# Attention with a feed-forward layer on one core: the scores' lower products on 64 rows, in pairs, and the last six products in two parts

## The chip, the cores and the metric

The kernel runs on one core of a Trainium2 chip. The metric is the device time of one execution in microseconds (us). Before the change three runs took 1043.27 to 1043.53 us, with a median of 1043.49.

The core's engines each work through their own queue in program order and wait for one another through semaphores: TensorE (PE; its weight loads are listed apart as PEld), VectorE (DVE), ScalarE (ACT), GpSimd (POOL), and SyncE (SP), which issues the DMAs.

## The reference

```python
# q, k, v: 8 batches x 8 heads x 576 positions x 64, float32
scores = scale * np.matmul(q, k.transpose(0, 1, 3, 2))      # scale = 1/8
mask = block_i >= block_j                                   # blocks of 64 positions
scores = np.where(mask, scores, -1000000000.0)
scores = scores - np.max(scores, axis=-1, keepdims=True)
attn = np.exp(scores)
attn = attn / (np.sum(attn, axis=-1, keepdims=True) + 1e-09)
attn_out = np.matmul(attn, v)
# heads side by side: x is 4608 x 512; w_in 512 x 2048, w_out 2048 x 512
h = x @ w_in
g = h * (1.0 / (1.0 + np.exp(-h)))
out = g @ w_out
```

So it is block-causal attention, and behind it a feed-forward layer (FFN) with a silu, on all 4608 tokens.

## The kernel before, in words

**Precision.** PE multiplies numbers of a rounded type, fp32r. To keep more digits, an operand is split in two: the upper part is the number rounded to fp32r, the lower part is what rounding left out. A product then is a sum of up to four: upper by upper, upper by lower, lower by upper, lower by lower.

**The first 128 queries** of each head are handled ahead, in large groups (classes First and Second; L524, L538, L576, L594), with small unrounded products on 64 rows or 64 columns of the PE array. They stand in the first 125 us, between weight preparation and the first FFN products. `warm` (L434) is filler for PE while the first data arrive.

**The units.** The other 448 queries of a head make one *unit*; there are 64 units, 8 batches by 8 heads. A unit's inputs are q and k transposed, 64 rows (the head dimension) by 448 + 576 columns. `load` fetches them twice, into partitions 0 to 63 and again into 64 to 127 (tile `raw`). `split_hi` (L278, ACT) rounds all of it into `qh`. `split_lo` (L282, POOL) then replaces k's columns in partitions 64 to 127 by k's lower part, so that k has its upper part in the lower half of the rows and its lower part in the upper half (`kk`). It also makes `ql`, the lower part of q, in both halves (L284).

**Scores** (L306, PE). A unit's scores are five areas, one per block of 128 keys (the fifth has 64), listed in `SEG` as (key block, column in the score row, first query, queries): 448, 320, 192, 448 and 64 queries wide, in three PSUM banks (`BANKS`). Each area is two products on all 128 rows: `kk` by `qh`, and `kk` by `ql`. With k's two parts in the two halves of the rows, the first gives upper by upper and lower by upper in one go, the second upper by lower and lower by lower. `QK` sets the order of the areas; an area's two products follow one another.

**Behind the scores** VectorE takes maxima (L250), subtracts them (L336, L338) and, behind ScalarE's exponentials, sums; ScalarE and GpSimd split the exponentials into `ph` and `pl`; PE multiplies them by v (L385), and the result becomes FFN input, again split.

**FFN.** Tokens go in 18 blocks of 256 (`TB`), the 2048 hidden columns in 8 steps of 256. `ffn1` (L618) makes 24 products of 256 columns per step, ScalarE applies silu (L625) and rounds (L631), GpSimd makes the lower part (L636), and `ffn2` (L648) makes 6 products of 512 columns for each half `t` of the block's tokens, summed over the 8 steps in one PSUM bank. In the last step `output` (L656) copies the bank into a tile `ot`, and `store` (L661) sends it to memory through SP.

**The order of the work** is written out by hand: a table of tokens for the start and the first 17 units, then a loop that emits each later unit with a number of FFN products between its parts. PE therefore alternates between a unit's scores, a unit's product with v, and FFN products. The last FFN products run after all units, with nothing beside them.

Of the kernel before, what the change touches and what calls it, by code (L numbers as in the profile page):

```python
# [9 lines left out]
F32 = mybir.dt.float32  # L10
# [4 lines left out]
ALU = mybir.AluOpType  # L15
# [3 lines left out]
B, H, S, D = 8, 8, 576, 64  # L19
DM, DFF = 512, 2048  # L20
P = 128
NQ = S - 2 * D
# [4 lines left out]
NFF = DFF // P  # L27
NSTEP = NFF // 2
TB = 256
CT = DM // P  # L30
NX = 16
EVEN = 4
# [5 lines left out]
SEG = [(0, 0, 0, 448), (2, 448, 128, 320), (3, 768, 256, 192), (1, 960, 0, 448), (4, 1408, 384, 64)]  # L38
COLS = 1472

QK = [0, 1, 3, 2, 4]
PV = [(0, 0, 128), (1, 0, 128), (2, 0, 128), (2, 1, 64), (1, 1, 64), (0, 1, 64), (4, 0, 128), (3, 1, 64), (3, 0, 128)]
BANKS = [(0, 448), (448, 960), (960, 1472)]

# [86 lines left out]
def attn_ffn(ctx: ExitStack, tc: tile.TileContext, qk, v, qk0, v0, qk1, v1, w_in, w_out, out):  # L131
    nc = tc.nc
# [5 lines left out]
    def bank(i):  # L138
        return pS.tile([P, 512], F32, tag=f"S{i}", name=f"S{i}")

    pU = pool("pU", space=PSUM)
    pH = pool("pH", bufs=2, space=PSUM)
    pO = pool("pO", bufs=2, space=PSUM)


    wi = [cp.tile([P, CT, DFF], F32R, name=f"wi{t}") for t in range(2)]
    wo = [cp.tile([P, NFF, DM], F32R, name=f"wo{t}") for t in range(2)]
# [10 lines left out]

    xbuf = cp.tile([P, NX, 2, TB], F32R, name="x")
    x_free = list(range(NX))  # L160
# [3 lines left out]
    ready = set()  # L164
# [96 lines left out]
    class Unit:  # L261
# [17 lines left out]

        def split_lo(u):  # L280

            nc.gpsimd.tensor_tensor(out=u.qh[64:, NQ:], in0=u.raw[64:, NQ:], in1=u.qh[64:, NQ:], op=ALU.subtract)  # L282
            u.ql = sp.tile([P, 512], F32R, tag="ql", name="ql")[:, :NQ]
            nc.gpsimd.tensor_tensor(out=u.ql, in0=u.raw[:, :NQ], in1=u.qh[:, :NQ], op=ALU.subtract)  # L284
            u.kk = u.qh[:, NQ:]
# [9 lines left out]
        def scores(u):  # L295
            banks = [bank(0), bank(1), bank(2)]

            def ps(c, w, r=P):
                i = max(i for i in range(3) if BANKS[i][0] <= c)
                return banks[i][:r, c - BANKS[i][0] : c - BANKS[i][0] + w]  # L300

            u.ps = ps
            for j, c, q0, w in (SEG[i] for i in QK):
                m = min(P, S - j * P)
                for i, qq in enumerate((u.qh, u.ql)):
                    nc.tensor.matmul(u.ps(c, w, m), u.kk[:, j * P : j * P + m], qq[:, q0 : q0 + w], start=i == 0, stop=i == 1)  # L306

        def max(u):
            ttr(Mx[:, :, 0], blocks32(u.ps(0, NQ)), ALU.max)
            for j, c, q0, w in SEG[1:4]:  # L310
                ttr(Mx[:, q0 // 32 + 2 :, j], blocks32(u.ps(c + 64, w - 64)), ALU.max)
                if j == 3:
                    u.half_max(0)
            u.half_max(1)
# [88 lines left out]
        def pieces(u):  # L403

            q = 0
            while q < NQ:
                blk, col = divmod(u.b * NQ + q, TB)
                n = min(TB - col, NQ - q)
                z = 4 + blk, u.h // 2
# [30 lines left out]
    class Early:  # L440
# [33 lines left out]
        def turn(u, k):  # L474
            for c in range(CT):
                nc.tensor.transpose(u.ps[k][:, P * c : P * c + P], u.part(k)[:, P * c : P * c + P], ident)
# [4 lines left out]
        def tiles(u, blk, n):  # L481

            for c in range(CT):
                if (blk, c) not in x_tiles:
# [3 lines left out]
            t = x_tiles[blk, 0]  # L488
            assert [x_tiles[blk, c] for c in range(CT)] == list(range(t, t + CT))
            return xbuf[:, t : t + CT]  # L490

    class First(Early):
# [18 lines left out]
        def scores(u):  # L511
# [6 lines left out]
            for k in range(2):  # L518
                for c in range(CT):
                    for e, b in enumerate(HALF):  # L520
# [19 lines left out]
        def hi(u, n):  # L540
            if n == 0:
                u.x = u.tiles(u.g, TB).rearrange("p c i (k n q) -> p i n k c q", k=2, n=2)
            nc.scalar.copy(u.x[:, 0, n], u.ps[n].rearrange("p (k c q) -> p k c q", k=2, c=CT))
# [61 lines left out]
    hs, gs, outs = {}, {}, {}  # L605

    def ffn1(blk, d, f):
        if f == 0:
            hs[blk, d] = pH.tile([P, 2, TB], F32, tag="h", name="h")
        h = hs[blk, d]  # L610
        n = 0
        for c in range(CT):
            x = xbuf[:, x_tiles[blk, c]]
            w = slice((2 * d + f) * P, (2 * d + f + 1) * P)
            assert x_full[blk, c] == TB, (blk, d, c, x_full[blk, c])
            assert ("in", d, c // 2) in ready
# [21 lines left out]
    def ffn2(blk, d, t):  # L638
        g2 = gs[blk, d]
        if d == 0 and t == 0:  # L640
            outs[blk] = [bank(2), pU.tile([P, DM], F32, tag="U", name="o1")] if blk == 0 else [pO.tile([P, DM], F32, tag="o", name="o") for _ in range(2)]
        o = outs[blk][t]
        tk = slice(t * P, t * P + P)
        n = 0
        for f in range(2):
            assert ("out", d, f) in ready
            for gt, wt in ((0, 0), (0, 1), (1, 0)):
                nc.tensor.matmul(  # L648
                    o, g2[:, gt, f, tk], wo[wt][:, 2 * d + f, :],
                    start=d == 0 and n == 0, stop=d == NSTEP - 1 and n == 5,  # L650
                )
                n += 1

    def output(blk, d, t):
        ot = sp.tile([P, DM], F32, tag="ot", name="ot", bufs=2)
        (nc.vector.tensor_copy if late else nc.scalar.copy)(ot, outs[blk][t])  # L656
        outs[blk][t] = ot

    def store(blk, d, t):
        for i, r, w in rows(blk, t):  # L660
            nc.sync.dma_start(out=out[r : r + w, :], in_=outs[blk][t][i : i + w, :])  # L661

    def rows(blk, t):

        if blk < 4:
            return [(i * D, (blk % 2 * 4 + t * 2 + i) * S + blk // 2 * D, D) for i in range(2)]
        r, i = [], 0
        while i < P:
            b, q = divmod((blk - 4) * TB + t * P + i, NQ)
            w = min(P - i, NQ - q)  # L670
            r.append((i, b * S + 2 * D + q, w))
            i += w
        return r


    steps = [(0, 0)] + [z for d in range(EVEN) for z in ((0, d + 1), (1, d))]
    steps += [(0, d) for d in range(EVEN + 1, NSTEP)] + [(1, d) for d in range(EVEN, NSTEP)]
    steps += [(blk, d) for blk in range(2, B * S // TB) for d in range(NSTEP)]


    work_list = []
    for n in range(len(steps) + LAG):
        now = n < len(steps)
        work_list += [("ffn", ffn1, n, f) for f in range(2) if now]
        if n < LAG:
            work_list += [("silu", silu, n), ("g_hi", g_hi, n), ("g_lo", g_lo, n)]
        else:
            last = steps[n - LAG][1] == NSTEP - 1
            for t in range(2):
                work_list += [("ffn", ffn2, n - LAG, t)] + [("output", output, n - LAG, t), ("store", store, n - LAG, t)] * last  # L690
                if now:
                    work_list += [[("silu", silu, n)], [("g_hi", g_hi, n), ("g_lo", g_lo, n)]][t]
    queues = {k: [z for z in work_list if z[0] == k] for k in ("ffn", "silu", "g_hi", "g_lo", "output", "store")}
    late = []
# [36 lines left out]
    for token in ORDER.split():  # L731
        name, _, method = token.partition(".")
        if name.startswith("warm:"):
            warm(int(name[5:]))
        elif method:
            method, _, k = method.partition(":")
# [5 lines left out]
    n = len(units)  # L742
    for i in range(TABLE, n + 2):
        u = units[i] if i < n else None
        w = units[i - 1] if i <= n else None
# [81 lines left out]
```

## Time and profile before

| | |
|---|---|
| median of 3 runs | 1043.49 us |
| the profiled execution's own time | 1043.46 us |
| its span (first to last instruction) | 1041.7 us |
| PE busy | 1033.4 us, 99% |
| weight loads (PEld) busy | 939.7 us, 90% |
| VectorE, ScalarE, GpSimd busy | 763.5, 749.1, 750.0 us |
| DMA | 79.95 MB, mean 77 GB/s |
| scores (L306), two groups | 90.5 and 84.1 us, 320 products each |
| FFN (L618, L648) | 441.6 and 424.3 us |

In a line of a group, the count follows the x; then come the busy time in us, the mean of one instruction in ns, and the idle time of the engine just before such instructions, with what ended it. In a timeline line the first number is the start in us from the span's start, the second the length, followed by engine, line, operation, output and input names, and the shape; for a matmul the first pair (128\*128) is the rows and columns of the array in use and the second the streamed operand. A matmul's recorded length includes its way through the array, so that lengths overlap; the distance between two starts is what it takes from PE. Times of PEld are those of the weight loads, which may run while PE is busy with the product before.

### The profile page before, as it was taken

How to read it: one execution, taken by the hardware profiler on the slowest of the kernel's cores; microseconds unless marked ns; L12 is line 12 of the kernel's file. 1: busy time of each engine (PE TensorE's matmuls, PEld its weight loads, DVE VectorE, ACT ScalarE, POOL GpSimd, SP SyncE). 2: the span in 40 equal slices, each digit the busy share in tenths (PEclk: the TensorE clock that was granted, in tenths of full speed). 3: DMA queues.
4: the chain of work that ended last, by engine and by line, in shares of the span. 5: the costliest groups of instructions: out<-in, count | busy, mean ns of one | idle time of the engine just before them, and what ended most of it. 6: DMA issues, size and time to landing. Idle time of an engine off the chain costs nothing.

```text
span 1041.7 us, 20247 instructions
## 1 busy us (share of the span) xinstructions
PE 1033.4 (99%) x7176; PEld 939.7 (90%) x7176; DVE 763.5 (73%) x2232; ACT 749.1 (72%) x1194; POOL 750.0 (72%) x726
## 2 busy tenths in 40 slices
PE   8999999999999999999999999999999999999998
PEld 8988899999899999999999999998999999989987
DVE  7998489999978988888878888888888888700000
ACT  5876578898797888787878787878787777722222
POOL 5766579898897878787878787878787878622221
PEclk9999999999999999999999999999999999999999
DMA  8876223222322222222322222222222222000000
GB/s 291 260 247 189 63 75 90 52 67 74 92 50 84 54 54 74 55 77 59 85 56 74 59 75 55 64 64 54 74 54 75 54 74 54 27 1 21 1 21 21
DMA packets 35044, 79.95 MB, mean 77 GB/s; under 512 B 4736, under 2 KB 12928, under 8 KB 34944
## 3 DMA queue, kind: packets, MB, share of 16 engines
q1 hardware_dynamic: 34944, 78.66, 26.9%
q8 instruction: 57, 0.93, 0.4%
q14 instruction: 43, 0.35, 0.1%
HBM read 69.21 MB, written 9.44 MB: 75 GB/s over the span
## 4 chain that ended last, share of the span: by engine, by line
PE 87%; DVE 4%; POOL 3%; ACT 2%; DMA 2%; issue 1%; SPq 0%; DVEq 0%; POOLq 0%; ACTq 0%
PE h L618 35%; PE o L648 35%; PE S L306 8%; PE U L385 8%; DVE S L227 1%; DVE wm L233 1%; DVE S L223 1%; DMA wst<-in_moe_w_in_dram 1%; POOL pl L361 1%; POOL g L636 1%; DMA T<-in_moe_w_in_dram 0%; PE S L648 0%; ACT L625 0%; DMA qkraw<-in_qk_dram 0%; POOL qh L282 0%
## 5 line engine op out<-in xcount | busy, mean ns | idle before, releaser
L618 PE MATMUL h<-x,wi 128*128 128x256 f32 x3456 | 441.6, 282 | 0.9 <-ACT g L625 0.6
L618 PEld LDWEIGHTS h<-x,wi 128*128 128x128 f32 x3456 | 430.2, 189 | 12.7 <-ACT g L625 1.0
L648 PE MATMUL o<-wo,g 128*128 128x512 f32 x1680 | 424.3, 397 | 0.0
L648 PEld LDWEIGHTS o<-wo,g 128*128 128x128 f32 x1680 | 305.9, 188 | 62.6 <-issue 0.2
L361 POOL TENSOR_TENSOR pl<-p,ph 128x448 fp32r<-128x448 f32 (+1 forms) x192 | 226.0, 1202 | 93.9 <-ACT ph L353 93.5
L636 POOL TENSOR_TENSOR g<-g,g 128x512 fp32r<-128x512 f32 x144 | 186.4, 1295 | 119.8 <-ACT g L631 115.2
L250 DVE TRANSPOSE_TENSOR_REDUCE Mx<-S 64x4 f32<-64x128 f32 (+4 forms) x384 | 135.7, 405 | 94.0 <-PE S L306 93.9
L625 ACT ACTIVATE g<-h 128x512 f32<-128x512 f32 x144 | 86.1, 598 | 126.0 <-POOL g L636 74.6
L631 ACT CAST g<-g 128x512 fp32r<-128x512 f32 x144 | 89.3, 620 | 60.1 <-PE o L648 58.2
L250 DVE TRANSPOSE_TENSOR_REDUCE Dx<-p 128x14 f32<-128x448 f32 (+3 forms) x320 | 122.6, 446 | 0.1
L347 ACT ACTIVATE p<-T 128x512 f32<-128x512 f32 (+1 forms) x192 | 105.6, 604 | 9.5 <-POOL ph L363 8.5
L353 ACT CAST ph<-p 128x512 fp32r<-128x512 f32 (+1 forms) x192 | 104.4, 596 | 1.3 <-PE U L385 1.1
L282 POOL TENSOR_TENSOR qh<-qkraw,qh 64x576 fp32r<-64x576 f32 x64 | 91.6, 1431 | 15.8 <-ACT qh L278 7.1
L306 PE MATMUL S<-qh 128*128 128x448 f32 (+3 forms) x320 | 90.5, 296 | 0.0
L625 ACT ACT_TABLE_LOAD x66 | 84.7, 1283 | 1.4 <-PE h L618 0.3
L306 PE MATMUL S<-ql,qh 128*128 128x448 f32 (+3 forms) x320 | 84.1, 307 | 0.0
L347 ACT ACT_TABLE_LOAD x62 | 79.5, 1283 | 1.6 <-DVE Dx L250 0.5
L284 POOL TENSOR_TENSOR ql<-qkraw,qh 128x448 fp32r<-128x448 f32 x64 | 74.1, 1157 | 5.1 <-PE S L594 0.2
L385 PE MATMUL U<-ph,vc 128*128 128x448 f32 (+3 forms) x320 | 74.1, 297 | 0.0
L278 ACT CAST qh<-qkraw 128x1024 fp32r<-128x1024 f32 x64 | 66.9, 1045 | 8.8 <-PE S L306 4.1
L338 DVE TENSOR_TENSOR T<-S,MR 128x256 f32<-128x256 f32 (+2 forms) x192 | 73.0, 406 | 0.0
L293 POOL TENSOR_TENSOR vc<-vraw,vc 128x320 fp32r<-128x320 f32 x64 | 56.2, 878 | 13.3 <-ACT vc L290 12.8
(120 smaller groups left out, 1120.4 us busy)
## 6 DMA issues: line engine op xcount, KB each, us to landing
qkraw<-in_qk_dram SPq DMA_DIRECT2D x128, 256.0 KB, 3.9
vraw<-in_v_dram SPq DMA_DIRECT2D x64, 160.0 KB, 2.3
wst<-in_moe_w_out_dram SPq DMA_DIRECT2D x15, 512.0 KB, 4.6
out_dram<-ot SPq DMA_DIRECT2D x24, 256.0 KB, 2.9
wst<-in_moe_w_in_dram SPq DMA_DIRECT2D x10, 512.0 KB, 5.3
v<-in_v_dram SPq DMA_DIRECT2D x12, 256.0 KB, 5.2
qk<-in_qk_dram SPq DMA_DIRECT2D x8, 384.0 KB, 5.3
T<-in_moe_w_in_dram SPq DMA_DIRECT2D x6, 512.0 KB, 4.5
```

Source lines behind the costliest of these rows:

```text
L250: nc.vector.tensor_reduce(out=out, in_=in_, axis=AX.X, op=op, apply_transpose=True)
L282: nc.gpsimd.tensor_tensor(out=u.qh[64:, NQ:], in0=u.raw[64:, NQ:], in1=u.qh[64:, NQ:], op=ALU.subtract)
L306: nc.tensor.matmul(u.ps(c, w, m), u.kk[:, j * P : j * P + m], qq[:, q0 : q0 + w], start=i == 0, stop=i == 1)
L347: nc.scalar.activation(u.p[:, c:e], T[:, c:e], AF.Exp, scale=SCALE)
L353: nc.scalar.copy(u.ph[:, c:e], u.p[:, c:e])
L361: nc.gpsimd.tensor_tensor(out=u.pl[:, c:e], in0=u.p[:, c:e], in1=u.ph[:, c:e], op=ALU.subtract)
L385: nc.tensor.matmul(U[:m, q0 : q0 + w], u.vc[:, j, :m], (u.ph, u.pl)[pp][:, c : c + w], start=n == 0, stop=n == 8)
L618: nc.tensor.matmul(h[:, f, :], wi[wt][:, c, w], x[:, xt, :], start=n == 0, stop=n == 3 * CT - 1)
L625: nc.scalar.activation(g, hs.pop((blk, d)), AF.Silu)
L631: nc.scalar.copy(g2[:, 0], g)
L636: nc.gpsimd.tensor_tensor(out=g2[:, 1], in0=g, in1=g2[:, 0], op=ALU.subtract)
L648: nc.tensor.matmul(o, g2[:, gt, f, tk], wo[wt][:, 2 * d + f, :], start=d == 0 and n == 0, stop=d == NSTEP - 1 and n == 5,)
```

## The change

It has two parts.

*Scores.* The second product of an area leaves out k's lower part: it multiplies only k's upper part by `ql`, on 64 of the 128 rows. For key blocks 0 and 1 k's upper part now lies in rows 64 to 127 (and the lower part in rows 0 to 63), for blocks 2 to 4 the other way round as before; `split_lo` writes the lower part accordingly, in two instructions. The new `QK` lists (area, part) and puts areas in pairs, one of blocks 0 and 1 with one of blocks 2 and 3: first both upper products on 128 rows, then both lower products, one on the upper 64 rows and the other on the lower 64, into different banks. The last area (64 keys) keeps both products on all rows. Lower by lower is left out of the sum for the first four areas.

*The end.* The last six products of the whole program, 512 columns wide, become six of columns 0 to 255 into the old bank and six of columns 256 to 511 into another. The old bank is copied to `ot` after the first six, and its left half can be stored; the right half's last products are then added by VectorE and stored apart.

```diff
-QK = [0, 1, 3, 2, 4]
+QK = [(0, 0), (1, 0), (0, 1), (1, 1), (3, 0), (2, 0), (3, 1), (2, 1), (4, 0), (4, 1)]
...
         def split_lo(u):
-            nc.gpsimd.tensor_tensor(out=u.qh[64:, NQ:], in0=u.raw[64:, NQ:], in1=u.qh[64:, NQ:], op=ALU.subtract)
+            for r, c in ((slice(0, 64), slice(NQ, NQ + 2 * P)), (slice(64, 128), slice(NQ + 2 * P, 1024))):
+                nc.gpsimd.tensor_tensor(out=u.qh[r, c], in0=u.raw[r, c], in1=u.qh[r, c], op=ALU.subtract)
...
-            for j, c, q0, w in (SEG[i] for i in QK):
+            for i, part in QK:
+                j, c, q0, w = SEG[i]
                 m = min(P, S - j * P)
-                for i, qq in enumerate((u.qh, u.ql)):
-                    nc.tensor.matmul(u.ps(c, w, m), u.kk[:, j * P : j * P + m], qq[:, q0 : q0 + w], start=i == 0, stop=i == 1)
+                r = u.upper(j) if part and m == P else slice(0, P)
+                qq = u.ql if part else u.qh
+                nc.tensor.matmul(u.ps(c, w, m), u.kk[r, j * P : j * P + m], qq[r, q0 : q0 + w], start=part == 0, stop=part == 1)
+
+        def upper(u, j):
+            return slice(64, 128) if j < 2 else slice(0, 64)
...
     def ffn2(blk, d, t):
...
+        split = t and (blk, d) == (NBLK - 1, NSTEP - 1)
+        if split:
+            outs[blk][t] += [(bank(0)[:, :HD], slice(HD, DM))]
+        for i, (o, c) in enumerate(outs[blk][t]):
+            if split and i == 0:
+                o, c = o[:, :HD], slice(0, HD)
...
     def output(blk, d, t):
         ot = sp.tile([P, DM], F32, tag="ot", name="ot", bufs=2)
-        (nc.vector.tensor_copy if late else nc.scalar.copy)(ot, outs[blk][t])
-        outs[blk][t] = ot
+        (o, c), *right = outs[blk][t]
+        (nc.vector.tensor_copy if late else nc.scalar.copy)(ot, o)
+        outs[blk][t] = [(ot, c)]
+        for o, c in right:
+            nc.vector.tensor_tensor(out=ot[:, c], in0=o, in1=ot[:, c], op=ALU.add)
+            outs[blk][t] = [(ot, slice(0, HD)), (ot, c)]

     def store(blk, d, t):
-        for i, r, w in rows(blk, t):
-            nc.sync.dma_start(out=out[r : r + w, :], in_=outs[blk][t][i : i + w, :])
+        for ot, c in outs[blk][t]:
+            for i, r, w in rows(blk, t):
+                nc.sync.dma_start(out=out[r : r + w, c], in_=ot[i : i + w, c])
```

On PE, one unit's scores in the middle of the program stood in this order before; `S_...` is a PSUM bank (three numbers, three banks), and the shape is the output's, keys by queries:

```order
L306 MATMUL S_4660<-qh 128x448
L306 MATMUL S_4660<-ql,qh 128x448
L306 MATMUL S_4661<-qh 128x320
L306 MATMUL S_4661<-ql,qh 128x320
L306 MATMUL S_4662<-qh 128x448
L306 MATMUL S_4662<-ql,qh 128x448
L306 MATMUL S_4661<-qh 128x192
L306 MATMUL S_4661<-ql,qh 128x192
L306 MATMUL S_4662<-qh 64x64
L306 MATMUL S_4662<-ql,qh 64x64
```

The same unit on PE after the change:

```order
L313 MATMUL S_4681<-qh 128x448
L313 MATMUL S_4682<-qh 128x320
L313 MATMUL S_4681<-ql,qh 128x448
L313 MATMUL S_4682<-ql,qh 128x320
L313 MATMUL S_4683<-qh 128x448
L313 MATMUL S_4682<-qh 128x192
L313 MATMUL S_4683<-ql,qh 128x448
L313 MATMUL S_4682<-ql,qh 128x192
L313 MATMUL S_4683<-qh 64x64
L313 MATMUL S_4683<-ql,qh 64x64
```

Still ten products of the same widths; the third and fourth, and the seventh and eighth, are the pairs on 64 rows, each into two banks.

At the end of the program, PE's last products before (`wo_75`, `wo_76` are the two parts of w_out):

```order
L648 MATMUL o<-wo_75,g_12894 128x512 x2
L648 MATMUL o<-wo_76,g_12894 128x512
L648 MATMUL o<-wo_75,g_12894 128x512 x2
L648 MATMUL o<-wo_76,g_12894 128x512
L648 MATMUL o<-wo_75,g_12894 128x512
```

And after the change:

```order
L669 MATMUL o<-wo_75,g_12958 128x512
L669 MATMUL o<-wo_75,g_12958 128x256
L669 MATMUL o<-wo_76,g_12958 128x256
L669 MATMUL o<-wo_75,g_12958 128x256 x2
L669 MATMUL o<-wo_76,g_12958 128x256
L669 MATMUL o<-wo_75,g_12958 128x256
L669 MATMUL S_12982<-wo_75,g_12958 128x256
L669 MATMUL S_12982<-wo_76,g_12958 128x256
L669 MATMUL S_12982<-wo_75,g_12958 128x256 x2
L669 MATMUL S_12982<-wo_76,g_12958 128x256
L669 MATMUL S_12982<-wo_75,g_12958 128x256
```

Six products became twelve of half the width, the later six into another bank.

More of the change, by code (lines that the diff above doesn't have):

```diff
@@ L29 @@
 TB = 256
+NBLK = B * S // TB
+HD = DM // 2
 CT = DM // P
@@ L640, in ffn2 @@
         if d == 0 and t == 0:
-            outs[blk] = [bank(2), pU.tile([P, DM], F32, tag="U", name="o1")] if blk == 0 else [pO.tile([P, DM], F32, tag="o", name="o") for _ in range(2)]
-        o = outs[blk][t]
-        tk = slice(t * P, t * P + P)
[L644 to L652, printed above, removed]
+            new = lambda: pO.tile([P, DM], F32, tag="o", name="o")
@@ new lines, in ffn2 @@
+            whole = slice(0, DM)
+            if blk == 0:
+                outs[blk] = [[(bank(2), whole)], [(pU.tile([P, DM], F32, tag="U", name="o1"), whole)]]
+            else:
+                outs[blk] = [[(new(), whole)] for _ in range(2)]
+        tk = slice(t * P, t * P + P)
+        split = t and (blk, d) == (NBLK - 1, NSTEP - 1)
[4 more added lines that the diff above has]
+                o, c = o[:, :HD], slice(0, HD)
+            n = 0
+            for f in range(2):
+                assert ("out", d, f) in ready
+                for gt, wt in ((0, 0), (0, 1), (1, 0)):
+                    nc.tensor.matmul(
+                        o, g2[:, gt, f, tk], wo[wt][:, 2 * d + f, c],
+                        start=(d == 0 or i > 0) and n == 0, stop=d == NSTEP - 1 and n == 5,
+                    )
+                    n += 1
@@ L677, in attn_ffn @@
     steps += [(0, d) for d in range(EVEN + 1, NSTEP)] + [(1, d) for d in range(EVEN, NSTEP)]
-    steps += [(blk, d) for blk in range(2, B * S // TB) for d in range(NSTEP)]
+    steps += [(blk, d) for blk in range(2, NBLK) for d in range(NSTEP)]
     work_list = []
```

## The prediction

> **What bounds the kernel now.** I read the page of the profile first, then the list of PE's waits, then PE's timeline around one unit's scores in the middle of the run. The page's rows give the span, the busy times, the granted clock, and the scores and what reads them.
>
> ```profile
> span 1041.7 us, 20247 instructions
> PE 1033.4 (99%) x7176; PEld 939.7 (90%) x7176; DVE 763.5 (73%) x2232; ACT 749.1 (72%) x1194; POOL 750.0 (72%) x726
> ...
> PEclk9999999999999999999999999999999999999999
> ...
> L250 DVE TRANSPOSE_TENSOR_REDUCE Mx<-S 64x4 f32<-64x128 f32 (+4 forms) x384 | 135.7, 405 | 94.0 <-PE S L306 93.9
> ...
> L306 PE MATMUL S<-ql,qh 128*128 128x448 f32 (+3 forms) x320 | 84.1, 307 | 0.0
> ```
>
> PE is busy for 99% of the span at full granted clock. A busy PE need not be at its peak, so the waits matter more. VectorE waits 94 us for the scores; the other way round there is nothing: before its scores PE has 0.0 us of idle. All of PE's waits, largest first:
>
> ```profile
> PE idle L434 <- DVE zero L429: 1.0, 1, 1.0
> PE S L576 <- PE h L618: 1.0, 1, 1.0
> PE h L618 <- ACT g L625: 0.6, 1, 0.6
> ```
>
> None is for an input of L306, L385 or L648. So while the 64 units run, PE's own stream sets the time, and each nanosecond that a unit's scores get longer or shorter goes into the span as it is. The other engines, at 72 to 73%, follow.
>
> The price of the scores is read from distances between starts (a matmul's recorded length overlaps the next one's). This is PE's timeline of one unit; column 1 is the start, column 2 the length.
>
> ```profile
> 509.24 0.36 PE L306 MATMUL S<-qh 128*128 128x448 f32 x1
> 509.44 0.36 PE L306 MATMUL S<-ql,qh 128*128 128x448 f32 x1
> 509.64 0.31 PE L306 MATMUL S<-qh 128*128 128x320 f32 x1
> 509.79 0.31 PE L306 MATMUL S<-ql,qh 128*128 128x320 f32 x1
> 509.94 0.36 PE L306 MATMUL S<-qh 128*128 128x448 f32 x1
> 510.14 0.37 PE L306 MATMUL S<-ql,qh 128*128 128x448 f32 x1
> 510.35 0.25 PE L306 MATMUL S<-qh 128*128 128x192 f32 x1
> 510.43 0.28 PE L306 MATMUL S<-ql,qh 128*128 128x192 f32 x1
> 510.55 0.19 PE L306 MATMUL S<-qh 128*64 128x64 f32 x1
> ```
>
> A product of 448 columns takes a slot of 0.20 us, one of 320 takes 0.15, the two of 192 take 0.20 together. The weights come free, as PEld's rows of the same place show: the load for the second product starts with the first product, on the same rows of the array, and is done before its turn.
>
> ```profile
> 509.24 0.19 PEld L306 LDWEIGHTS S<-ql,qh 128*128 128x128 f32 x1
> 509.44 0.19 PEld L306 LDWEIGHTS S<-qh 128*128 128x128 f32 x1
> ```
>
> **What the pairs save.** Of each unit's ten products, four (448 with 320, 448 with 192) now use 64 rows each and can run two at a time. That two halves of the rows do run together is seen in the early blocks, whose products have 64 rows (PE's timeline; S and U of one step are the upper and the lower rows on the same columns):
>
> ```profile
> 6.27 0.22 PE L524 MATMUL U<-qk 64*64 64x64 f32 x1
> 6.31 0.22 PE L524 MATMUL S<-qk 64*64 64x64 f32 x1
> 6.31 0.22 PE L524 MATMUL U<-qk 64*64 64x64 f32 x1
> 6.32 0.22 PE L524 MATMUL S<-qk 64*64 64x64 f32 x1
> 6.33 0.22 PE L524 MATMUL U<-qk 64*64 64x64 f32 x1
> 6.47 0.27 PE L434 MATMUL idle<-zero 128*64 128x64 f32 x1
> ```
>
> Four start within 0.02 us, into two banks, and the group before ended its starts at 6.27: four per 0.06 us. So a pair should cost its longer member. That saves the slot of 320 columns, 0.15, and one of 192. The two 192s take 0.20 together; the one that stays needs about 0.09 (192 of 448 columns of 0.20), so 0.11 goes. Together 0.26 us per unit.
>
> **What the pairs cost.** The order of a unit is now: two products on 128 rows, a pair on 64, two on 128, a pair on 64, then two on 128 again (the 64-key block keeps all rows). That is four changes between 128 and 64 rows per unit, where there was none. The trace has such changes where early blocks stand between FFN products. PE, then PEld, at the first of them, and PE's timeline inside and after its block:
>
> ```profile
> 28.25 0.87 PE L618 MATMUL h<-x,wi 128*128 128x256 f32 x6
> ```
> ```profile
> 29.05 0.85 PEld L576 LDWEIGHTS S<-qk 64*64 64x64 f32 x16
> 30.07 0.41 PEld L618 LDWEIGHTS h<-x,wi 128*128 128x128 f32 x3 [0.17 <-issue]
> ```
> ```profile
> 29.05 0.33 PE L576 MATMUL S<-qk 64*64 64x128 f32 x2
> ```
> ```profile
> 29.43 0.71 PE L576 MATMUL S<-qk 64*64 64x128 f32 x10
> ```
> ```profile
> 30.07 0.38 PE L618 MATMUL h<-x,wi 128*128 128x256 f32 x1
> ```
> ```profile
> L618 PE MATMUL h<-x,wi 128*128 128x256 f32 x3456 | 441.6, 282 | 0.9 <-ACT g L625 0.6
> ...
> L576 PE MATMUL S<-qk 64*64 64x128 f32 x128 | 8.7, 275 | 1.4 <-PE h L618 1.0 <-DVE x L602 0.4
> ```
>
> Six L618 products span 0.87 us; less the last one's 0.28 they start 0.118 apart, the last at 28.84. The next would follow at 28.96. Instead, even the weight load comes only at 29.05: 0.09 late, and not ahead of its product any more. Going back is alike: ten L576 products are five pairs in 0.71 us; less 0.27, pairs start 0.11 apart, the last at 29.87. The next slot is 29.98, but the load starts at 30.07, 0.09 late again, and its product is recorded 0.38 long instead of 0.28: it waits another 0.10 for 128 columns of weights. (Into the block it was 0.32 to 0.27, 0.05, for 64 columns.) So a change costs 0.09 plus the bare weight load, 0.10: **0.19 us**.
>
> Those blocks halve the columns too; is it the rows? The row 6.33 above, with 6.47 behind it, changes rows from 64 to 128 and keeps 64 columns: 0.14 between starts where the slot is 0.06, 0.08 late. So a change of rows alone pays it, though no row of before has exactly 128x128 to 64x128. The Trainium skill ("TensorEngine Tiling (Array Packing)", section Tiling Modes) states that a change of tiling mode, not of tile alone, drains TensorE. It gives no price; the rows just quoted agree, and by that rule all four changes of a unit pay.
>
> Per unit: into and out of the first pair and into the second, 3 x 0.19; out of the second pair the next weights have 64 columns, 0.09 + 0.05 = 0.14. That is 0.71. Less the 0.26 saved: +0.45 us, and times 64 units **+28.8 us**. Nothing hides this, for PE waits for no one. Bounds per unit: if the pairs' two loads expose only 0.05 each, as for L576, 0.35, or 22.4 us. If a pair's members take turns, nothing is saved, 0.71, or 45.4 us.
>
> **The other edits.** GpSimd's subtraction of 64x576 becomes 256 and 320 columns. GpSimd's rows:
>
> ```profile
> L282 POOL TENSOR_TENSOR qh<-qkraw,qh 64x576 fp32r<-64x576 f32 x64 | 91.6, 1431 | 15.8 <-ACT qh L278 7.1
> ...
> L284 POOL TENSOR_TENSOR ql<-qkraw,qh 128x448 fp32r<-128x448 f32 x64 | 74.1, 1157 | 5.1 <-PE S L594 0.2
> ...
> L293 POOL TENSOR_TENSOR vc<-vraw,vc 128x320 fp32r<-128x320 f32 x64 | 56.2, 878 | 13.3 <-ACT vc L290 12.8
> ```
>
> From the last two, 128 columns more cost 279 ns, 2.18 each, so 180 ns are fixed. A second instruction adds 0.18 us per unit, 11.5 us of GpSimd's time, while PE never waits for it and its queue has idle time; at most it moves g's and p's lower parts 0.18 us in a unit that itself grows 0.45. I take 0; without that cover it would be the whole 11.5 us. VectorE gets its first block later by the 320 product's slot and the change (0.15 + 0.19 = 0.34 us), again less than the unit grows, so no new wait forms there.
>
> The end, on PE, ScalarE, SP and, for the price of an add of that shape, VectorE's group:
>
> ```profile
> 1037.63 0.63 PE L648 MATMUL o<-wo,g 128*128 128x512 f32 x2
> ```
> ```profile
> 1038.29 0.58 ACT L656 COPY ot<-o 128x512 f32<-128x512 f32 x1 [0.82 <-PE o L648]
> ```
> ```profile
> L338 DVE TENSOR_TENSOR T<-S,MR 128x256 f32<-128x256 f32 x64 | 26.1, 409 | 0.0
> ```
>
> Now the copy of 0.58 runs beside the last six products (six of 256 columns, 6 x 0.118 = 0.71), and only an add of 256 columns, 0.41, follows the last product. Twelve products of 0.118 (L618's distance) stand for six of 0.23 (448 columns' 0.20 scaled to 512): even. In the row above, two of them end at 1038.26, and the copy follows at once. The gain is 0.17 us; the second store queues behind the first on SP, but the first is issued earlier. I take -0.15, with 0 and -0.5 as ends.
>
> **The sum.** The profiled run took 1043.46 us, 1.76 over its span and 0.03 under the median of 1043.49. 1043.46 + 28.8 - 0.15 = **1072.1 us, said as 1072**.
>
> **The rivals.**
> - *Pairs without drains.* If a change of rows alone on 128 columns costs nothing, each unit saves 0.26: 64 x 0.26 = 16.6 us, 1043.46 - 16.6 - 0.15 = 1026.7 us. It decides from 0.065 us per change (0.26 / 4): below that the kernel gains. For it: these operands are rounded (fp32r), those of L524, L434 and L576 are not, and where rounded products go from 128 to 64 columns, 510.43 to 510.55 in the unit, the distance is 0.12, hardly over the 192 columns' 0.09; changes of shape may be cheap for them. Against it: both halves of the rows must hold their own weights here, as at 6.31, and the way back from that cost 0.08 with the columns unchanged. The Trainium skill's table (same page, section Overview) gives up to twice the speed for a contraction of 64 and deducts nothing for getting there; by it this is the outcome. Chance 0.10.
> - *The pair takes turns.* Two full-width products at the rounded rate write twice as much into PSUM as L524's 64 columns did; if they alternate, drains stay and nothing is saved: 1043.46 + 45.4 - 0.15 = 1088.7 us. Chance 0.09.
> - *Weights slip in under the drain.* Only 4 x 0.09 paid: +0.10 per unit, 6.4 us, 1049.7 us. Against it: loads at 29.05 and 30.07 start with the drain's end. Chance 0.03.
> - *Nothing changes in the array:* 64 rows run as 128 with half idle, in turn and without drain: 1043.3 us. Against it: S and U side by side at 6.31. Chance 0.02.
>
> **The numbers.** The forecast of 1072 holds 0.76, mostly between 1064 and 1078. The range must take in the turn-taking pair to leave out no more than 2 in 10: 1063 to 1089. A difference of 0.2%, about 2 us, is what a measurement of this kernel can tell from none. Faster by more 0.10, same 0.02, slower 0.88.
>
> **What would show it.** In the changed kernel's timeline: loads of a pair starting 0.09 after the last slot, both members within 0.01, the first product behind a pair recorded 0.10 longer, a unit's period 0.45 longer, PE's busy share and PEld's falling a little, and still no wait of PE for another engine. The prediction is wrong if the loads of the pair start with the product ahead of them, if members start 0.15 or more apart, or if PE waits for VectorE or GpSimd.

## The result, and the profile after

The changed kernel takes 1071.2 us (median of 4 runs, 1071.05 to 1072.36), the kernel before 1043.51 beside it. The ratio is 1.0266, 95% interval 1.0254 to 1.0279: 27.7 us slower. The forecast was 1072.

The page of the changed kernel, in the rows that answer to those of before:

```profile
span 1069.3 us, 20315 instructions
PE 1062.4 (99%) x7182; PEld 918.5 (86%) x7182; DVE 765.3 (72%) x2233; ACT 750.6 (70%) x1194; POOL 758.9 (71%) x790
...
PEclk9999999999999999999999999999999999999999
...
L253 DVE TRANSPOSE_TENSOR_REDUCE Mx<-S 64x4 f32<-64x128 f32 (+4 forms) x384 | 136.5, 406 | 117.8 <-PE S L313 117.7
...
L287 POOL TENSOR_TENSOR qh<-qkraw,qh 64x256 fp32r<-64x256 f32 (+1 forms) x128 | 102.9, 804 | 18.5 <-ACT qh L281 9.2
```

PE is still at 99% and at full clock, VectorE waits 118 us for the scores instead of 94, and GpSimd's line has the 11 us more that its second instruction was priced at (102.9 us in L287, 91.6 in L282 before). The busy share of PE hides the loss: a product that waits for its weights is recorded longer and counts as busy. PEld's fall from 90 to 86% is no measure of it either: the two loads of a pair now run side by side (below), which by estimate takes 128 x 0.19 = 24 us out of PEld's busy time (939.7 to 918.5 us). Of the kernels tried below, one_island has 922.2 us of PEld with hardly any loss, and alone has 949.4 with the largest. PE's list of waits, of which these are the first two lines, names no score input:

```profile
PE idle L445 <- DVE zero L440: 1.0, 1, 1.0
PE S L587 <- PE h L629: 1.0, 1, 1.0
```

One unit in the changed kernel, PE's timeline; a row of x2 holds two products, and its shape is the first one's. The last two rows are single products from narrower windows: the first one behind the first pair, and the next unit's first one:

```profile
523.60 0.51 PE L313 MATMUL S<-qh 128*128 128x448 f32 x2
524.04 0.46 PE L313 MATMUL S<-ql,qh 64*128 64x448 f32 x2
524.43 0.56 PE L313 MATMUL S<-qh 128*128 128x448 f32 x2
524.92 0.46 PE L313 MATMUL S<-ql,qh 64*128 64x448 f32 x2
525.32 0.24 PE L313 MATMUL S<-qh 128*64 128x64 f32 x1
525.40 0.22 PE L313 MATMUL S<-ql,qh 128*64 128x64 f32 x1
525.45 0.72 PE L629 MATMUL h<-x,wi 128*128 128x256 f32 x4
...
524.43 0.47 PE L313 MATMUL S<-qh 128*128 128x448 f32 x1
...
536.74 0.36 PE L313 MATMUL S<-qh 128*128 128x448 f32 x1
```

and the weight loads of the same place:

```profile
524.03 0.19 PEld L313 LDWEIGHTS S<-ql,qh 64*128 64x128 f32 x2 [0.25 <-issue]
524.43 0.30 PEld L313 LDWEIGHTS S<-qh 128*128 128x128 f32 x2 [0.21 <-issue]
524.92 0.19 PEld L313 LDWEIGHTS S<-ql,qh 64*128 64x128 f32 x2 [0.20 <-issue]
525.32 0.13 PEld L313 LDWEIGHTS S<-qh 128*64 128x64 f32 x1 [0.21 <-issue]
```

At each of the four changes of rows the load column has a hole of 0.20 to 0.25 us in front of it, marked "issue": in that time PEld waits for nothing that the profile shows. Over all units the profile lists 253 such holes before L313's loads, 54.6 us together, and three more that end with GpSimd: 256, four times 64. Before L306's loads, in the kernel before, it lists none. Going in: the second product started at 523.80 (523.60 + 0.51 - 0.31), its slot ends at 523.95, the load comes at 524.03, 0.08 late. The pair's two loads start together (both fit into 0.19, the length of one) and so do its two products, both done by 524.50; the longer is recorded 0.46 long where 448 columns had 0.36, 0.10 for bare weights. The groups of all units, the members of 448 and of 320 columns, say the same of both:

```profile
L313 PE MATMUL S<-ql,qh 64*128 64x448 f32 x128 | 59.8, 467 | 0.0
L313 PE MATMUL S<-ql,qh 64*128 64x320 f32 x64 | 26.3, 410 | 0.0
```

Before, on 128 rows, these products had means of 365 and 309 ns: each member waits 0.10 us for its weights, none waits for the other. Coming out: 524.04 + 0.10 + 0.20 = 524.34 is the end of the pair's slot, the load comes at 524.43, 0.09 late, and the product behind it has 0.47, another 0.10 or 0.11.

In the kernel before, the unit behind the one that began at 509.24 began here:

```profile
521.93 0.36 PE L306 MATMUL S<-qh 128*128 128x448 f32 x1
```

So a unit took 521.93 - 509.24 = 12.69 us and now takes 536.74 - 523.60 = 13.14: +0.45, and 64 x 0.45 = 28.8 us. The loss lies among the units: from the first to the last start of their upper products it was 771.1 us (120.6 to 891.7), and it is 798.9 now (120.7 to 919.6).

### The profile page after: what moved, and what is told of

It is laid out like the page before. It is cut to its first block, busy times and chain, and to the rows that moved or that the text cites. A ratio compares the mean times of both kernels' runs of the same rounds, so it can differ in the third digit from the quotient of the medians.

```text
span 1069.3 us, 20315 instructions
## 1 busy us (share of the span) xinstructions
PE 1062.4 (99%) x7182; PEld 918.5 (86%) x7182; DVE 765.3 (72%) x2233; ACT 750.6 (70%) x1194; POOL 758.9 (71%) x790
## 4 chain that ended last, share of the span: by engine, by line
PE 91%; DVE 4%; DMA 1%; POOL 1%; issue 1%; ACT 1%; SPq 0%; DVEq 0%; ACTq 0%
PE h L629 36%; PE o L669 35%; PE S L313 11%; PE U L396 8%; DVE S L230 1%; DVE wm L236 1%; DVE S L226 1%; DMA wst<-in_moe_w_in_dram 1%; PE S L669 0%; DMA T<-in_moe_w_in_dram 0%; PE S L587 0%; POOL wi L213 0%; POOL wi L247 0%; DVE MR L466 0%; PE S L605 0%
## 5 line engine op out<-in xcount | busy, mean ns | idle before, releaser
L669 PE MATMUL o<-wo,g 128*128 128x512 f32 (+1 forms) x1680 | 423.1, 397 | 0.0
L287 POOL TENSOR_TENSOR qh<-qkraw,qh 64x256 fp32r<-64x256 f32 (+1 forms) x128 | 102.9, 804 | 18.5 <-ACT qh L281 9.2
L313 PE MATMUL S<-qh 128*128 128x448 f32 (+3 forms) x320 | 84.2, 328 | 0.0
L313 PEld LDWEIGHTS S<-qh 128*128 128x128 f32 (+1 forms) x320 | 49.4, 177 | 30.0 <-issue 27.0
L313 PE MATMUL S<-ql,qh 64*128 64x448 f32 (+3 forms) x320 | 74.1, 384 | 0.0
```

The source lines that it names most:

```text
L287: nc.gpsimd.tensor_tensor(out=u.qh[r, c], in0=u.raw[r, c], in1=u.qh[r, c], op=ALU.subtract)
L313: nc.tensor.matmul(u.ps(c, w, m), u.kk[r, j * P : j * P + m], qq[r, q0 : q0 + w], start=part == 0, stop=part == 1)
L669: nc.tensor.matmul(o, g2[:, gt, f, tk], wo[wt][:, 2 * d + f, c], start=(d == 0 or i > 0) and n == 0, stop=d == NSTEP - 1 and n == 5,)
```

## The experiments

**The theory** is that of the prediction: each change between 128 and 64 rows holds the next weight load back for 0.09 us (the prediction's drain) and leaves these weights bare (0.10 for 128 columns), and PE's stream is the bound. **Rival A**: the loss comes from two halves at work side by side. **Rival B**: it comes from what else moved, the order of products, VectorE's later start, GpSimd's second instruction. The first four kernels ran on one chip beside the kernel before, 1043.98 us there; the last three on one where it took 1043.64.

**No change of rows** (label all_rows):

```diff
-                r = u.upper(j) if part and m == P else slice(0, P)
+                r = slice(0, P)
```

> The changed kernel with its new order of products, its two GpSimd instructions and its new end, but every product on all 128 rows again (the lower products take in k's lower part again). Theory (changes between 128 and 64 rows cost 0.19 us each): without changes of rows nothing is lost, 1043.5 less 0.4 for the end = about 1043.1 us, at most 0.5 off. Rival A (the cost lies in two halves at work side by side, not in the change): no pair runs side by side, about 1043 too. Rival B (the cost lies in the new order, in VectorE's later start or in GpSimd's second instruction): all of that is still there, about 1071 us.

Measured 1043.98 us, ratio 1.0002 (0.9992 to 1.0012), no difference to the kernel beside it; the 0.4 us expected of the end do not show. The new order, the later first block and GpSimd's extra work cost nothing that can be measured. Rival B falls.

**Two changes per unit** (label one_island). Two areas now share a bank while both are unfinished, so only the first product into a bank carries the start flag:

```diff
-QK = [(0, 0), (1, 0), (0, 1), (1, 1), (3, 0), (2, 0), (3, 1), (2, 1), (4, 0), (4, 1)]
+QK = [(0, 0), (1, 0), (3, 0), (2, 0), (4, 0), (4, 1), (0, 1), (1, 1), (3, 1), (2, 1)]
...
-                nc.tensor.matmul(u.ps(c, w, m), u.kk[r, j * P : j * P + m], qq[r, q0 : q0 + w], start=part == 0, stop=part == 1)
+                nc.tensor.matmul(u.ps(c, w, m), u.kk[r, j * P : j * P + m], qq[r, q0 : q0 + w], start=part == 0 and i in (0, 1, 3), stop=part == 1 and i in (0, 2, 3))
```

> All upper products and the 64-key area's two products first, then both pairs one behind the other: two changes of rows per unit instead of four, same products, same pairs. Theory: 2 x 0.19 - 0.26 saved = +0.12 us per unit, x 64 = 7.7 us, less 0.4 at the end: about 1050.8 us (1049 to 1053). Rival A: the two pairs per unit are still there, about 1071 us. Rival B: VectorE gets its first block still later than in the changed kernel, 1071 us or more.

Measured 1045.76 us, ratio 1.0018 (1.0009 to 1.0027). Same products, same pairs, half the changes, and nearly all of the loss is gone: Rival A falls, the changes are what costs. But 1.8 us over before is less than the 7.3 expected, 0.09 us per unit too little. Where the rest went is the question of two runs below.

**Eight changes, no pair** (label alone):

```diff
-QK = [(0, 0), (1, 0), (0, 1), (1, 1), (3, 0), (2, 0), (3, 1), (2, 1), (4, 0), (4, 1)]
+QK = [(0, 0), (0, 1), (1, 0), (1, 1), (3, 0), (3, 1), (2, 0), (2, 1), (4, 0), (4, 1)]
```

> Areas in the order of before, each followed by its lower product on 64 rows, alone: eight changes of rows per unit, nothing side by side. Theory: 7 x 0.19 + 0.14 = 1.47 us per unit and nothing saved, x 64 = 94.1 us, less 0.4: about 1137 us (1125 to 1145). Rival A: no halves at work side by side, so no loss, 1043 to 1050 us. Rival B: the order is that of before, so at most GpSimd's share is left, under 1055 us.

Measured 1137.44 us, ratio 1.0901 (1.0885 to 1.0917): 93.5 us over before, 1.46 us per unit where 1.47 was expected. Its PE timeline, each row one product:

```profile
557.47 0.37 PE L313 MATMUL S<-qh 128*128 128x448 f32 x1
557.76 0.47 PE L313 MATMUL S<-ql,qh 64*128 64x448 f32 x1
558.16 0.41 PE L313 MATMUL S<-qh 128*128 128x320 f32 x1
558.50 0.41 PE L313 MATMUL S<-ql,qh 64*128 64x320 f32 x1
558.84 0.47 PE L313 MATMUL S<-qh 128*128 128x448 f32 x1
```

In these rows every product behind a change is recorded 0.10 longer than its like before (0.47 against 0.36 or 0.37, 0.41 against 0.31), and from one to the next of them 0.40 us pass for 448 columns (557.76 to 558.16) where the slot is 0.20: 0.19 to 0.20 per change, of which 0.10 are the bare weights, whether it goes to 64 rows or back.

**Pairs that take turns** (label same_half): k's upper part in rows 0 to 63 for all blocks.

```diff
-            for r, c in ((slice(0, 64), slice(NQ, NQ + 2 * P)), (slice(64, 128), slice(NQ + 2 * P, 1024))):
+            for r, c in ((slice(64, 128), slice(NQ, NQ + 2 * P)), (slice(64, 128), slice(NQ + 2 * P, 1024))):
...
-            return slice(64, 128) if j < 2 else slice(0, 64)
+            return slice(0, 64)
```

> The changed kernel, but k's upper part lies in rows 0 to 63 for all key blocks, so both members of a pair use the same 64 rows and have to take turns: four changes of rows as in the changed kernel, nothing side by side. Theory: 0.71 us per unit and the saving of 0.26 gone, x 64 = 45.4 us, less 0.4: about 1088.5 us (1084 to 1092), and in the trace a pair's members 0.13 to 0.20 us apart. Rival A: faster than the changed kernel, towards 1043 us. Rival B: same order and same GpSimd work, about 1071 us.

Measured 1086.9 us, ratio 1.0412 (1.0397 to 1.0428): 42.9 us over before, 15 more than the changed kernel's 27.7, which is 0.24 us per unit; the pairs' saving was put at 0.26. PE's first pair here, its first member alone, and the group of the 320-column members:

```profile
532.29 0.61 PE L313 MATMUL S<-ql,qh 64*128 64x448 f32 x2
...
532.29 0.47 PE L313 MATMUL S<-ql,qh 64*128 64x448 f32 x1
...
L313 PE MATMUL S<-ql,qh 64*128 64x320 f32 x64 | 19.4, 304 | 0.0
```

On one half the pair needs 0.61, on two halves 0.46. The second member, 304 ns long, has no bare weights here and starts 0.31 behind the first (532.29 + 0.61 - 0.30 = 532.60); the 0.13 to 0.20 expected had left out the 0.10 that the first one waits for its weights. The saving of the change was real.

**Why one island cost so little.** Behind the 64-key area's products the next weights are bare in the kernel before too. PE's last product of a unit of before, and the first FFN product behind it:

```profile
510.58 0.22 PE L306 MATMUL S<-ql,qh 128*64 128x64 f32 x1
510.63 0.36 PE L618 MATMUL h<-x,wi 128*128 128x256 f32 x1
```

The FFN product has 0.36 where its group's mean is 0.28: 0.08 us that the unit pays anyway. The rows suggest why: the product ahead gives it only 0.05 us (510.58 to 510.63), and a load of 128 columns of weights is recorded 0.19 long. **Theory M**: with the pairs right behind the 64-column products, this 0.08 and the bare weights of the change are one and the same. **Theory R**: two pairs in a row save more than two apart. To tell them apart, the 64-key products moved to the front of the unit, the pairs staying in one island (label short_first):

```diff
-QK = [(0, 0), (1, 0), (0, 1), (1, 1), (3, 0), (2, 0), (3, 1), (2, 1), (4, 0), (4, 1)]
+QK = [(4, 0), (4, 1), (0, 0), (1, 0), (3, 0), (2, 0), (0, 1), (1, 1), (3, 1), (2, 1)]
...
-                nc.tensor.matmul(u.ps(c, w, m), u.kk[r, j * P : j * P + m], qq[r, q0 : q0 + w], start=part == 0, stop=part == 1)
+                nc.tensor.matmul(u.ps(c, w, m), u.kk[r, j * P : j * P + m], qq[r, q0 : q0 + w], start=part == 0 and i != 2, stop=part == 1 and i != 1)
```

> As the kernel with one island per unit (which came out 1.8 us over before where 7.3 were expected), but the 64-key area's two products stand first in the unit and not right ahead of the pairs. Theory M (behind a 64-column product the next weights are bare anyway, 0.08 us, in the kernel before too; in front of the pairs that bareness and the pairs' own fell together and were paid once): now a product of 192 columns stands ahead of the pairs and nothing falls together, so 2 x 0.19 - 0.26 = +0.12 us per unit, 7.7 us, less 0.4 at the end: 7.3 us over before, 6 to 9. Theory R (the two halves of the rows run on by themselves, so two pairs in a row save more than two pairs apart): no difference to one island, 1 to 3 us over before.

Measured 1052.09 us, ratio 1.0083 (1.0067 to 1.0098): 8.5 us over before. Theory R falls. PE's and PEld's rows, the 64-key products first:

```profile
514.59 0.19 PE L313 MATMUL S<-qh 128*64 128x64 f32 x1
514.62 0.22 PE L313 MATMUL S<-ql,qh 128*64 128x64 f32 x1
514.68 0.45 PE L313 MATMUL S<-qh 128*128 128x448 f32 x1
```
```profile
515.49 0.19 PEld L313 LDWEIGHTS S<-ql,qh 64*128 64x128 f32 x2 [0.19 <-issue]
```

The first area now waits 0.09 (0.45 against 0.36) behind them, and the pairs' loads come bare once more behind the last upper product. The same from the other side, the smallest island that there can be, in the kernel before (label small_island):

```diff
-                    nc.tensor.matmul(u.ps(c, w, m), u.kk[:, j * P : j * P + m], qq[:, q0 : q0 + w], start=i == 0, stop=i == 1)
+                    r = slice(0, 64) if i and j == 4 else slice(0, P)
+                    nc.tensor.matmul(u.ps(c, w, m), u.kk[r, j * P : j * P + m], qq[r, q0 : q0 + w], start=i == 0, stop=i == 1)
```

> The kernel before with one edit: the very last product of a unit's scores, the 64-key area's lower one, runs on rows 0 to 63 (k's lower part left out of it). Two changes of rows per unit, no pair, nothing saved. Flat prices: 0.14 in (64 columns of weights) and 0.19 out, 0.33 us per unit, 21 us over before. Theory M: the way out falls together with the 0.08 to 0.10 us of bare weights that stand behind this product anyway, so about 0.23 us per unit, 15 us over before (12 to 17). Rival A (halves side by side cost, changes don't): no change, 0 to 3 us over before.

Measured 1057.94 us, ratio 1.0137 (1.0123 to 1.0151): 14.3 us over before, 0.22 us per unit; 0.23 by theory M, 0.33 by flat prices. Theory M also gives the size for one_island: 2 x 0.19 - 0.26 - 0.08 = 0.04 us per unit, 0.03 measured.

**The end alone** (label end_only), in the kernel before:

```diff
+        split = t and (blk, d) == (NBLK - 1, NSTEP - 1)
...
```

with the rest of that part of the change, as shown in the section on the change; the scores are those of the kernel before.

> The kernel before with only the new end (last six products in two parts, an add, two stores). From the two traces, from the last product's start to the end of the span: 3.84 us before, 3.43 in the changed kernel. Expected 0.4 us under before, 0.04%, which a comparison may not tell from none; in the trace those 0.4 us at the end.

Measured 1043.68 us, ratio 0.9999 (0.9990 to 1.0008). No difference can be told from it. The rows of the changed kernel's end, PE and VectorE, and PE's of end_only:

```profile
1065.27 0.88 PE L669 MATMUL S<-wo,g 128*128 128x256 f32 x6
```
```profile
1066.24 0.42 DVE L681 TENSOR_TENSOR ot<-S,ot 128x256 f32<-128x256 f32 x1 [125.32 <-PE S L669]
```
```profile
1037.08 0.88 PE L668 MATMUL S<-wo,g 128*128 128x256 f32 x6
```

From the end of the last product (1066.15) to the end of the span (1069.3) it is 3.15 us; before, 1038.26 to 1041.7, 3.44; in end_only, 1037.96 to 1041.1, 3.14. That 0.3 us is seen in single profiles only; it was not shown by times.

The scores side of all runs in one table, per unit, over the kernel beside it (the whole difference divided by 64; expected is what was expected before the run, for small_island by theory M):

| kernel | changes | pairs side by side | expected, us | measured, us |
|---|---|---|---|---|
| all_rows | 0 | no | 0.00 | 0.00 |
| one_island | 2 | yes | 0.12 | 0.03 |
| short_first | 2 | yes | 0.12 | 0.13 |
| small_island | 2 | no | 0.23 | 0.22 |
| the changed kernel | 4 | yes | 0.45 | 0.43 |
| same_half | 4 | no | 0.71 | 0.67 |
| alone | 8 | no | 1.47 | 1.46 |

The changed kernel and same_half lie a little under their sums. In their profiles PE's busy time grew by 29.0 us (1033.4 to 1062.4) and 45.2 us (to 1078.6), where the sums were 28.8 and 45.4; PE's idle time shrank, from 8.3 us to 6.9 and 6.8.

No version was faster than the kernel before. An evener split of the areas over the two halves would bring two halves' products into one PSUM bank (areas 1 and 2 share one) and was not tried.

## Why the prediction was right

**The bound** held: PE waits for no input of the scores in the changed kernel, so what the unit gained in length went into the time, 0.45 us in the trace and 28.8 expected against 27.7 measured. VectorE and GpSimd followed, as all_rows shows by itself.

**The price of a change**, 0.09 for what the prediction calls the drain and 0.10 for bare weights, was read from blocks on 64 rows of another size and operand type, and stood in each of the four places (0.05 for the 64 columns of weights, 0.24 against 0.19 at 525.32). No row of before had 128x128 to 64x128 on rounded operands; that the price carried over to them was a bet, and it came out. What the array does in the 0.09 us no run shows: the rows show only that the next load starts that much after the slot. By the rule of the Trainium skill ("TensorEngine Tiling (Array Packing)", section Tiling Modes) all four changes pay; the loads at 524.03, 524.43, 524.92 and 525.32 agree, each behind a hole. The Trainium skill's table of gains (same page, section Overview) gives up to twice and deducts nothing for getting there. Here the pair taken alone went from 0.61 to 0.46, bare weights in both, and the unit as a whole lost.

**The saving**, 0.26 us, measured 0.24. So the rival of pairs without drains, 1026.7 us, failed on the changes, and that of turn-taking pairs, 1088.7 us, on the pair; same_half, which takes turns by design, then measured 1086.9, close to the latter's number. Weights slipping in under the drain, 1049.7 us, failed on the 0.47 at 524.43, and an array in which nothing changes, 1043.3 us, on the two products that start together at 524.04.

**Mis-sized in a small way**: the end was put at -0.15 us and shows 0.3 in the trace: 0.1 from the add (done 0.51 behind the last product, the copy before 0.61), the rest behind it, where the last store carries 128 KB instead of 256 (at the end 1.7 us from issue to landing in the median against 2.0). PE's busy share did not fall as said: a product that waits for weights counts as busy. PEld's fell, but for the pairs' loads side by side. And the flat price per change has an exception that the prediction did not see, right behind a product of 64 columns; in the changed kernel no change of rows stands there, so the sum did not suffer.

## What to carry to other kernels

Count the changes between 128 and 64 rows as well as the columns saved: here each costs about the slot of a 448-column product (0.19 to 0.20 us), so a pair must save more than it takes to get in and out. If narrow products are wanted, put them in one run, and lay its edge against a product that already leaves the next weights bare; here even that only came near the kernel before (1.8 us over). An engine that is busy for 99% can still lose time inside its instructions: compare distances between starts and the weight loads' holes.

## What the runs showed that was not expected

A very short product ahead of a change made the change cheaper: a unit of one_island took 0.10 us less than one of short_first (1.8 and 8.5 us over before, by 64), though both have two changes and the same products. The two halves also did not get in each other's way: in the mean of all units the member of 448 columns took 467 ns in a pair and 466 in alone, that of 320 took 410 and 407. And each half goes on by itself: in one_island the product of 192 columns starts 0.05 us before the one of 448 that stands ahead of it in the program but on the other half.
